# First batch of an FFT and FFN kernel: filter rows interleaved over the partitions, two filter units loaded twice, one product moved to GpSimd

## Chip, cores, metric

One core of one Trainium2 chip. The metric is the device time of one execution in microseconds (us); every time below is a median of several executions. Positions such as "at 38.09" are us from the start of the span of one profiled execution. SyncE, GpSimd, VectorE, ScalarE and TensorE are the engines; SPq in a profile is the instruction queue of SyncE, which here only issues DMA transfers.

## The reference, cut

```python
X = np.fft.rfft(x, axis=1)                       # x: 8 x 3008 x 256, float32
Y = X * (filt_r + 1j * filt_i)[None]             # filters: 1505 x 256 each, float32
y = np.fft.irfft(Y, n=3008, axis=1).reshape(24064, 256)
h = y @ w_in                                     # w_in: 256 x 2048
g = h * (1.0 / (1.0 + np.exp(-beta * h)))
out = g @ w_out                                  # w_out: 2048 x 256
```

## The kernel before, the parts that matter

The FFT is done as matmuls against tables that the kernel builds. The filtered spectrum of the first batch is made in six units of four frequency columns (`KU = 4`, `NUN = 6`). Each unit is matmuls (`s2_0`), two products on VectorE with the filters, and 16 more matmuls (`s3_0`, called by `unit`). Only when all six units are through can the FFN of the first batch start; from there TensorE runs to the end almost without a gap (0.84 us, the wait for xg). Filters are loaded once by SyncE, into one half of the 128 partitions, and copied to the other half by GpSimd (`spread`). Behind those copies, in the same GpSimd queue, stand the loads of w_in, and then of the second batch's rows (`load_x`, tile `xg`). The loads of w_out (tile `ws`) follow the filters in SyncE's queue.

```python
    def load_filters(k0, k1):                    # M = 64, H = 32
        n = k1 - k0
        for filt, dst, p0 in ((filt_r, fr_sb, M), (filt_i, fi_sb, 0)):
            for q0, off, sg in ((p0, k0, 1), (p0 + H, N1 - k0, -1)):
                src = AP(filt.tensor, filt.offset + off * D, [[N1 * D, H], [sg * D, n], [1, D]])
                nc.sync.dma_start(dst[q0 : q0 + H, k0:k1, :], src)
    # ... cut
    for u in range(NUN):
        load_filters(u * KU, (u + 1) * KU)
    # ... cut
    def s2_0(u):
        # ... cut: matmuls into ps
        nc.vector.tensor_tensor(pq[u, 0][:], ps[:], fr_sb[:, ks, :], ALU.mult)
        nc.vector.scalar_tensor_tensor(pq[u, 1][:], ps[:], rot[:], fi_sb[:, ks, :], ALU.mult, ALU.mult)
    # ... cut
    def spread(u):
        ks = slice(u * KU, (u + 1) * KU)
        nc.gpsimd.tensor_copy(fr_sb[:M, ks, :], fr_sb[M:, ks, :])
        nc.gpsimd.tensor_copy(fi_sb[M:, ks, :], fi_sb[:M, ks, :])
    # ... cut
    for u in range(4):
        spread(u)
    load_win(0, 4 * P)
    spread(4)
    load_win(4 * P, FF)
    spread(5)
    for g in range(4):
        load_x(1, g)
```

## Time and profile before

| | before |
|---|---|
| time | 782.33 us (782.07 to 782.78) |
| TensorE busy, whole span | 764.1 of 780.2 us |
| last of the 24 filter loads issued / landed | 22.29 / 26.70 |
| w_in loads issued | 23.40 and 26.37 |
| last product of the first batch ended | 30.61 |
| first FFN matmul | 33.84 |

### The profile page before, as it was taken

The numbers are of one execution on the slowest core, as the hardware profiler recorded it, in microseconds if no ns is written. First come the engines' busy times: TensorE is split into PE (matmuls) and PEld (weight loads), VectorE is DVE, ScalarE is ACT, GpSimd is POOL, SyncE is SP. The second block draws the span as 40 slices with busy tenths as digits, with TensorE's granted clock in tenths as the row PEclk, the third lists the DMA queues.
The fourth block names the chain that finished last, engine by engine and source line by source line (L and its number), as shares of the span: only waits on it lengthen the run. The fifth ranks groups of instructions, "written<-read, shape, count | busy, mean of one in ns | idle before, by whom it ended". The sixth has DMA issues, their size and how long they took to land.

```text
span 780.2 us, 15154 instructions
## 1 busy us (share of the span) xinstructions
PE 764.1 (98%) x5956; PEld 544.0 (70%) x6051; DVE 446.0 (57%) x713; ACT 552.6 (71%) x814; POOL 151.4 (19%) x155
## 2 busy tenths in 40 slices
PE   8899999999999999999999999999999999999997
PEld 5677667766776667866678666776667776676665
DVE  7869754766556665566546665567655666321001
ACT  6767877676677766777667776677766777777776
POOL 6714400312012210122201322022200222000000
PEclk9999999999999999999999999999999999999999
DMA  9975585244913358042671417622164111500101
GB/s 185 233 213 116 147 209 155 70 108 115 252 42 80 103 116 242 29 113 71 152 207 45 119 48 181 176 75 69 48 189 135 48 48 49 156 28 28 55 28 55
DMA packets 84411, 88.51 MB, mean 113 GB/s; under 512 B 5788, under 2 KB 74652, under 8 KB 84340
## 3 DMA queue, kind: packets, MB, share of 16 engines
q1 hardware_dynamic: 79892, 73.81, 32.0%
q0 software_dynamic: 4304, 13.60, 10.5%
q8 instruction: 47, 0.77, 0.4%
q14 instruction: 24, 0.20, 0.1%
q10 hardware_dynamic: 144, 0.13, 0.0%
HBM read 54.47 MB, written 46.66 MB: 130 GB/s over the span
## 4 chain that ended last, share of the span: by engine, by line
PE 94%; DMA 2%; issue 1%; POOL 1%; DVE 1%; SPq 0%; ACT 0%; DVEq 0%; POOLq 0%
PE acc L788 43%; PE hps L770 39%; PE ps L561 3%; PE ps L629 3%; PE ps L607 3%; PE ps L577 2%; DMA xg<-in_x_dram 1%; DMA fi_sb<-in_filt_i_dram 1%; POOL fi_sb L473 0%; POOL fr_sb L472 0%; SPq L91 0%; PE ps L405 0%; PE tp L400 0%; DVE y L114 0%; DVE u L224 0%
## 5 line engine op out<-in xcount | busy, mean ns | idle before, releaser
L779 ACT ACTIVATE gT<-hps,beta_sb 128x512 bf16<-128x512 f32 x752 | 516.9, 687 | 213.3 <-PE hps L770 191.9
L788 PE MATMUL acc<-wout_sb,gT 128*128 128x256 bf16 x3008 | 452.9, 272 | 2.3
L770 PE MATMUL hps<-y,win_sb 128*128 128x512 bf16 (+7 forms) x1636 | 428.0, 350 | 0.1
L788 PEld LDWEIGHTS <-gT 128*128 128x128 bf16 x3008 | 286.9, 98 | 121.6 <-issue 0.9
L596 POOL TENSOR_TENSOR yh<-a_t,b_t 128x512 bf16<-128x512 f32 x84 | 106.4, 1267 | 424.1 <-DVE b_t L595 422.8
L770 PEld LDWEIGHTS <-win_sb 128*128 128x128 bf16 x1728 | 164.8, 98 | 25.2 <-issue 0.9
L112 DVE COPY ost<-acc 128x512 f32<-128x512 f32 (+1 forms) x94 | 59.9, 679 | 138.3 <-PE acc L788 138.2
L112 DVE CAST a<-ps 96x512 bf16<-96x512 f32 x107 | 72.9, 685 | 53.3 <-PE ps L561 49.3
L114 DVE TENSOR_SCALAR y<-ps 128x376 bf16<-128x376 f32 (+2 forms) x128 | 63.3, 510 | 61.2 <-PE ps L629 57.9
L591 DVE TENSOR_TENSOR a_t<-ps,fr_sb 128x512 f32<-128x512 f32 x84 | 58.1, 692 | 67.0 <-PE ps L577 66.5
L592 DVE SCALAR_TENSOR_TENSOR b_t<-ps,fi_sb 64x512 f32<-64x512 f32 x84 | 58.2, 693 | 1.1
L595 DVE TENSOR_TENSOR b_t<-ps,fi_sb 64x512 f32<-64x512 f32 x84 | 57.4, 683 | 1.1
L112 DVE CAST z<-ps 128x512 bf16<-128x512 f32 x72 | 49.3, 684 | 1.7 <-PE ps L607 0.8
L629 PEld LDWEIGHTS <-zz 96*128 96x128 bf16 x448 | 29.7, 97 | 22.9
L561 PE MATMUL ps<-xg,t 94*96 94x512 bf16 x112 | 41.9, 381 | 1.5 <-DMA xg<-in_x_dram 0.8
L629 PE MATMUL ps<-t,zz 96*128 96x94 bf16 x448 | 34.7, 205 | 0.7
L607 PE MATMUL ps<-yh,t 128*128 128x256 bf16 x168 | 32.1, 273 | 0.6
L577 PE MATMUL ps<-a,t 128*128 128x256 bf16 x168 | 32.1, 273 | 0.3
L607 PEld LDWEIGHTS <-t 128*128 128x128 bf16 x168 | 16.2, 98 | 17.7 <-issue 0.7
L577 PEld LDWEIGHTS <-t 128*128 128x128 bf16 x168 | 16.1, 98 | 16.3
L171 POOL DMA_DIRECT2D xg<-in_x_dram x24 | 12.5, 521 | 56.7 <-PE ps L561 56.7
L561 PEld LDWEIGHTS <-t 94*96 94x96 bf16 x112 | 13.8, 123 | 10.3
(95 smaller groups left out, 177.3 us busy)
## 6 DMA issues: line engine op xcount, KB each, us to landing
out_dram<-ost SPq DMA_DIRECT2D x42, 512.0 KB, 3.0
d<-a SPq DMA_DIRECT2D x28, 384.0 KB, 5.1
a<-d SPq DMA_DIRECT2D x28, 384.0 KB, 4.9
d<-z SPq DMA_DIRECT2D x28, 384.0 KB, 3.9
zz<-d SPq DMA_DIRECT2D x28, 384.0 KB, 7.1
xg<-in_x_dram POOLq DMA_DIRECT2D x24, 384.0 KB, 6.3
out_dram<-ost SPq DMA_DIRECT2D x9, 256.0 KB, 3.8
ws<-in_moe_w_out_dram SPq DMA_DIRECT2D x4, 512.0 KB, 6.6
```

The source lines that it names most:

```text
L112: nc.vector.tensor_copy(dst, src)
L114: nc.vector.tensor_scalar_mul(dst, src, scale)
L561: nc.tensor.matmul(ps[:KP], lhsT=t1[:], rhs=xg[b, g][:NP, jj : jj + 2, :], start=True, stop=True)
L577: nc.tensor.matmul(ps[:, e, :], lhsT=t2[:, k0 + e, :], rhs=st["a2", b, g][:, kk + e, :], start=True, stop=True,)
L591: nc.vector.tensor_tensor(a_t[:], ps[:], fr_sb[:, ks, :], ALU.mult)
L592: nc.vector.scalar_tensor_tensor(b_t[:M], ps[M:], -1.0, fi_sb[M:, ks, :], ALU.mult, ALU.mult)
L596: nc.gpsimd.tensor_tensor(yh[:], a_t[:], b_t[:], ALU.add)
L607: nc.tensor.matmul(ps[:, e, :], lhsT=t3[:, 2 * i + e, :P], rhs=yh[:, e, :], start=True, stop=True)
L629: nc.tensor.matmul(ps[:, e, :NP], lhsT=zz[:, j0 % JG + e, dc * P : (dc + 1) * P], rhs=t4[:], start=True, stop=True,)
L770: nc.tensor.matmul(hps[:, pos - t0 : pos - t0 + ln], lhsT=win_sb[:, dc, fb * P : (fb + 1) * P], rhs=ys[b][:, dc, n0 : n0 + ln], start=(dc ...
L779: nc.scalar.activation(gT[:], hps[:], ACT.Silu, scale=beta_sb[:, fb : fb + 1])
L788: nc.tensor.matmul(acc_of(i, tb)[:, tb % 2, :], lhsT=blk[i * NFB + fb][:, tb * P : (tb + 1) * P], rhs=wout_sb[:, fb, :], start=(fb == 0 an ...
```

## The change

Its intent, as far as the code tells: write each filter load to every second of 64 partitions in place of 32 neighbouring ones (the frequency rows k and their mirrored rows are interleaved; the tables are reordered to match), take real and imaginary loads in turn, load the last two units straight into both halves so that GpSimd need not copy them and can issue w_in and xg earlier, give one product of the fifth unit to GpSimd, and shift the second batch's first steps by one so that TensorE meets xg later. The order of the calls of the units, and of the scaling of w_out on GpSimd, changes with it.

```diff
+    DUP = 2 * KH
+    def load_filters(k0, k1, halves):
+        for hi, off, sg in ((0, k0, 1), (1, N1 - k0, -1)):
+            for (filt, dst), p0 in zip(FILTERS, halves):
+                src = AP(filt.tensor, filt.offset + off * D, [[N1 * D, H], [sg * D, k1 - k0], [1, D]])
+                nc.sync.dma_start(dst[p0 + hi : p0 + M : 2, k0:k1, :], src)
 # ... cut: tables reordered, t2_shift by exclusive-or on pairs
-    for u in range(NUN):
-        load_filters(u * KU, (u + 1) * KU)
+    for u in range(DUP // KU):
+        load_filters(u * KU, (u + 1) * KU, (M, 0))
+    load_filters(DUP, NK, (M, 0))
+    load_filters(DUP, NK, (0, M))
 # ... cut
+        if on_pool:
+            nc.scalar.activation(zc[:], ps[:], ACT.Copy, scale=rot[:])
         nc.vector.tensor_tensor(pq[u, 0][:], ps[:], fr_sb[:, ks, :], ALU.mult)
+        if on_pool:
+            return
 # ... cut
     load_win(0, 4 * P)
-    spread(4)
     load_win(4 * P, FF)
-    spread(5)
-    for g in range(4):
-        load_x(1, g)
+    load_x(1, 0)
 # ... cut: order of the calls below
+    s2_0(4, True)
+    pool_product(4)              # two gpsimd.tensor_tensor of 128x512
+    for g in range(1, 4):
+        load_x(1, g)
 # ... cut: second batch
-            s1_steps(1, range(16), [1 + (2 * i + 1) // 3 for i in range(16)], False, (1, 4, 7, 10, 13))
-            for i, r in enumerate((11, 12, 13, 14)):
+            s1_steps(1, range(16), [2 + (2 * i + 1) // 3 for i in range(16)], False, (1, 4, 7, 10, 13))
+            for i, r in enumerate((2, 3, 4, 5)):
                 at(r, f_late, 1, i // 2, i % 2)
             for g in range(NG):
-                at(o + 13, a2_load, 1, g)
+                at(o + 14, a2_load, 1, g)
```

The number of filter loads stays 24: 16 of 128 KB for the first four units and 8 of 256 KB for the last two.

More of the change, by code (lines that the diff above doesn't have):

```diff
@@ L84 @@
     CH = M * J
-    def load_filters(k0, k1):
-        n = k1 - k0
-        for filt, dst, p0 in ((filt_r, fr_sb, M), (filt_i, fi_sb, 0)):
-            for q0, off, sg in ((p0, k0, 1), (p0 + H, N1 - k0, -1)):
-                src = AP(filt.tensor, filt.offset + off * D, [[N1 * D, H], [sg * D, n], [1, D]])
-                nc.sync.dma_start(dst[q0 : q0 + H, k0:k1, :], src)
+    FILTERS = ((filt_r, fr_sb), (filt_i, fi_sb))
+    DUP = 2 * KH
[4 more added lines that the diff above has]
+                nc.sync.dma_start(dst[p0 + hi : p0 + M : 2, k0:k1, :], src)
     t1 = consts.tile([NP, KP], BF16, name="t1", tag="t1")
@@ L184 @@
     load_x0(8, 16)
-    iota(vi[:, :, :H], [[1, NK], [N1, H]])
+    viv = vi[:].rearrange("p k (m h) -> p k m h", h=2)
+    iota(viv[:, :, :, 0], [[1, NK], [N1, H]])
     load_x0(16, 24)
-    iota(vi[:, :, H:], [[1, NK], [-N1, H]], base=N1 * (M - 1))
+    iota(viv[:, :, :, 1], [[1, NK], [-N1, H]], base=N1 * (M - 1))
     load_x0(24, 28)
@@ L218 @@
     q_i = shift_and("q_i", 0, 1)
-    v_i = shift_and("v_i", 5, 1)
     q_p = (affine("q0", q_i, -1.0, 1.0), affine("q1", q_i, 1.0, 0.0))
@@ L224, in t2_half @@
         nc.vector.tensor_scalar(
-            t[:], vi[:, :, hi * H : (hi + 1) * H], ms[:], off[:], ALU.mult, ALU.add
+            t[:], viv[:, :, :, hi], ms[:], off[:], ALU.mult, ALU.add
         )
@@ L228, in t2_half, with t2_shift @@
         nc.scalar.activation(
-            t2[:, :, hi * H : (hi + 1) * H], t[:], ACT.Sin, scale=TWO_PI / TURN
-        )
-    def t2_shift(hi):
-        for c in range(2):
+            t2[:, :, :M].rearrange("p k (m h) -> p k m h", h=2)[:, :, :, hi],
+            t[:],
+            ACT.Sin,
+            scale=TWO_PI / TURN
+        )
+    def t2_shift():
+        pairs = t2[:].rearrange("p k m -> p (k m)").bitcast(I32).rearrange("p (k m) -> p k m", k=NK)
+        for c, bit in enumerate((1 << 15, -(1 << 31))):
             d0, s0 = (0, M) if c == 0 else (M, 0)
-            dst = t2[d0 : d0 + M, :, M + hi * H : M + (hi + 1) * H]
-            src = t2[s0 : s0 + M, :, hi * H : (hi + 1) * H]
-            if c == hi:
-                nc.vector.tensor_scalar_mul(dst, src, -1.0)
-            else:
-                nc.vector.tensor_copy(dst, src)
+            nc.vector.tensor_scalar(
+                pairs[d0 : d0 + M, :, H:], pairs[s0 : s0 + M, :, :H], bit, None, ALU.bitwise_xor
+            )
     MG = 4
@@ L310 @@
     nc.sync.dma_start(seen[:], t2[:1, 1, M - 2 : M])
-    for u in range(NUN):
-        load_filters(u * KU, (u + 1) * KU)
+    for u in range(DUP // KU):
+        load_filters(u * KU, (u + 1) * KU, (M, 0))
+    load_filters(DUP, NK, (M, 0))
+    load_filters(DUP, NK, (0, M))
     gp = nc.gpsimd
-    rot = affine("rot", v_i, 2.0, -1.0, gp)
+    rot = affine("rot", q_i, 2.0, -1.0, gp)
     tiny = sp.tile([P, NFB], F32, name="tiny", tag="tiny")
@@ L321 @@
     spin(5, idle)
-    t2_shift(0)
-    t2_shift(1)
+    t2_shift()
     nc.vector.memset(t2[:, 0, M : P : M - 1], 0.0)
@@ L424, with s2_0 @@
     p0pool = rpool("p0pool", r_p0, bufs=2, **tw)
-    def s2_0(u):
+    zc = sr.tile([P, KU, D], F32, name="zc", tag="zc")
+    def s2_0(u, on_pool=False):
         ps = bank2([P, KU, D])
@@ L482, with pool_product @@
     load_win(0, 4 * P)
-    spread(4)
     load_win(4 * P, FF)
-    spread(5)
-    for g in range(4):
-        load_x(1, g)
+    load_x(1, 0)
+    def pool_product(u):
+        for i in range(0, KU, 2):
+            k0 = u * KU + i
+            nc.gpsimd.tensor_tensor(
+                pq[u, 1][:, i : i + 2, :], zc[:, i : i + 2, :], fi_sb[:, k0 : k0 + 2, :], ALU.mult
+            )
     load_wout(0)
     load_wout(WG)
-    scale_wout(0)
-    scale_wout(WG)
     s2_0(0)
@@ L500 @@
     s2_0(2)
+    a0_turn(4)
     unit(1)
-    a0_turn(4)
     s2_0(3)
+    a0_turn(5)
+    s2_0(4, True)
+    pool_product(4)
+    for g in range(1, 4):
+        load_x(1, g)
+    scale_wout(0)
+    scale_wout(WG)
     unit(2)
-    s2_0(4)
-    a0_turn(5)
     t3_part(2, True)
     t3_neg(2, True)
-    unit(3)
     s2_0(5)
@@ L512 @@
     spin(3, idle)
+    unit(3)
     unit(4)
```

## The prediction

> **What bounds the kernel now.** I read the stretches first (busy time of each engine in windows of the span), because shares over 780 us hide a short phase. Columns: window, its length, then busy us and count for PE, PEld, DVE, ACT, POOL, then the granted clock, DMA share, GB/s.
>
> ```profile
> 0.00:36.60 36.60, 30.08 (x340) 21.12 (x344) 30.29 (x56) 26.35 (x38) 27.26 (x41) 1.00 1.00 208
> 36.60:64.00 27.40, 27.18 (x231) 19.28 (x235) 19.30 (x42) 17.59 (x28) 3.79 (x2) 1.00 0.72 203
> 120.00:400.00 280.00, 278.21 (x2124) 198.09 (x2157) 175.24 (x271) 194.93 (x285) 51.95 (x49) 1.00 0.46 122
> ```
>
> From 36.6 us to the end TensorE has no idle time worth having (278.21 of 280). The change touches nothing there but the order of a few early pieces. So the time is "when does the steady stream begin" plus a constant, and the whole question is the first 36.6 us, where the DMA engines are full (share 1.00) while no compute engine is. Next the chain of waits, as start, length, what:
>
> ```profile
> 26.37 0.37 POOL win_sb L476
> 26.74 0.40 issue
> 27.14 1.03 POOL fr_sb L472
> 28.17 0.06 issue
> 28.23 0.39 POOL fi_sb L473
> 28.62 0.59 issue
> 29.21 7.35 DMA xg<-in_x_dram
> 36.56 0.04 issue
> 36.61 0.38 PE ps L561
> ```
>
> GpSimd copies the filters from one half of the partitions to the other (12 copies of 1.04 us), and behind the copies in its queue stand the loads of the FFN weights and of the second batch's rows (xg). xg is issued at 29.21, lands at 36.56, and TensorE waits 0.84 us for it at step 1. Beside it runs a second, nearly as long chain on VectorE, the two filter products of six units:
>
> ```profile
> 25.38 1.21 DVE L434 TENSOR_TENSOR pq_t<-sps,fr_sb 128x1024 bf16<-128x1024 f32 x1
> 26.52 1.27 DVE L435 SCALAR_TENSOR_TENSOR pq_t<-sps,rot,fi_sb 128x1024 bf16<-128x1024 f32 x1
> 28.20 1.22 DVE L434 TENSOR_TENSOR pq_t<-sps,fr_sb 128x1024 bf16<-128x1024 f32 x1 [0.41 <-POOL fr_sb L472]
> 29.34 1.27 DVE L435 SCALAR_TENSOR_TENSOR pq_t<-sps,rot,fi_sb 128x1024 bf16<-128x1024 f32 x1
> ```
>
> The products run back to back from 16.08, 2.32 us a unit, lose 0.41 us to the last GpSimd copy, and end at 30.61. The first FFN matmul follows at 33.84, and 2.7 us later TensorE stands before xg. Both chains must get shorter; either alone is worth at most the 0.84 us.
>
> Last, what the DMA engines do. The first line is the stretch from 15 to 24 us, filter loads alone; the second from 26 to 27 us, the load of w_out, 1 KB packets over 128 partitions:
>
> ```profile
> DMA packets 1510, 2.08 MB, mean 231 GB/s; under 512 B 250, under 2 KB 1254, under 8 KB 1510
> DMA packets 341, 0.33 MB, mean 334 GB/s; under 512 B 15, under 2 KB 341, under 8 KB 341
> ```
>
> Filters move at 231 GB/s although many of their packets are larger. In the packet records a 4 KB filter packet takes 159 ns when alone and about 300 ns in the crowded stretch; a 1 KB one 46 against about 70.[...]
>
> [...]
> [...]here GpSimd's 128x512 sum takes 1267 ns, and I use that.[...]
>
> **The change part by part.**
> 1. GpSimd loses four copies (units 4 and 5): 4 x 1.04 = 4.2 us before the x load. Copies of unit 3 still end near 23.4 to 23.9 (they follow the landing of the filters, 22.27 for unit 3), so both weight loads and the first x load (0.84 + 0.72 + 0.5) are issued by about 25.5 to 26 instead of 29.7. Since the DMA engines are full, the landing moves by less than the issue.
> 2. DMA gains 1.05 MB: units 4 and 5 twice. In units of 128 KB the filters go from 24 to 32. Before, these 24 took from about 12.0 to 25.7 us (one engine, about 1 us behind, ends at 26.7): 0.56 us each. Unchanged rate: 32 x 0.56 = 17.9, end 29.9, with the late engine 31, plus what the w_in load takes in between. At 300 GB/s (0.437 each): 14.0, end 26.0, late 27.0. At 382 (my ceiling from 2 x 159 + 8 x 46 ns for 16 KB on an engine): 11, end 23, late 24.
> 3. VectorE loses one 1.27 us product, unit 5's 0.41 us wait, and saves little in the table shift (two exclusive-ors on 64x768 words in place of four bf16 operations of 0.36 us; perhaps 0.1 to 0.2 us, hidden behind x arriving at 9.96). Six units then want to end at 16.08 + 6 x 2.32 - 1.14 = 28.9, if the filters are there.
> 4. ScalarE gains one scaled copy[...]; it has room, being idle 1.1 us before two later evacuations.
> 5. GpSimd gains two products of 1.27 us, 2.5 us, which need all the imaginary filters of unit 4, i.e. the last DMA of the filters. The first is ready at about 26.0 at best. They end at 28.6 (ceiling rate), at 29.6 (300 GB/s: 27.0 + 2.5), or at 33.6 and later (old rate).
> 6. TensorE meets xg one step later; a step without it (two matmuls of the first layer, 0.43, and eight transposes, 0.45) is 0.88 us, enough to cover the present wait of 0.84. The moved pieces load VectorE in steps 2 to 5 to about 1.9 us against 1.4 on TensorE; three PSUM buffers should absorb most of 2 us, so I put 0 to 0.4 us on it.
>
> Sum by filter rate, for the start of the steady stream, as the later of the product chain and xg. Ceiling: products end about 1.4 us earlier (after 28.6, two half units of matmul, 0.6 each), and the 0.85 us wait goes: -2.3. At 300: the products end about where they did (GpSimd at 29.6 to 30.0 holds up unit 4 and the last unit behind it), xg lands about 0.7 us later from the added bytes (14.0 against 13.3), and the step's shift gives 0.88: about -0.2 to -0.6. At 236: unit 4 waits to about 30, GpSimd to 33.6 or more, the start slips by 4.5 to 5, less 0.85: about +3.9.
>
> **The rivals.**
> (a) The added bytes cost more than GpSimd's copies: filters still at 231 to 245 GB/s, the last load after 30 us, a new VectorE wait on DMA before unit 4, time 784 to 786.[...] Against it: 4 KB packets did run at 159 ns in the first microsecond[...]; and nobody would buy 1 MB more without room.
> (b) Filters run near the ceiling, so that the x load lands by about 35 and the product chain sets the start: 780.0. For it: w_out ran at 334 GB/s right after.[...]
> (c) The GpSimd product becomes the last link: 2.5 us on an engine twice as slow as the 1.27 us it replaces. At middle rates this eats the gain, time 781.5 to 782.3. For it: it depends on the very last load. Against it: unit 4 is not the last unit, so about 1.2 us of slack lies behind VectorE's own last product.
> (d) Later effects (steps 2 to 5) give back up to 0.4 us; small.
>
> **Range and chances.** I expect a rate of 300 to 330 GB/s[...] and so -1.0 us: 781.3 us. The best case worked out above is -2.3 (780.0), the worst plausible +3.9 (786.2); I take 779.3 to 785.0 as eight in ten. 2% is 15.6 us; no rival comes near it, since the whole stage touched is 36.6 us and nothing in it is worth 15: 0.98 for within 2%, 0.01 each side.
>
> **What would show it.** Right: mean GB/s from 15 to 24 us above 290; no wait of unit 4's product for fr_sb over 0.5 us; win_sb issued before 24.5 and xg before 26; the TensorE wait for xg gone or under 0.3 us; first FFN matmul before 33.9; the rest unchanged in length. Wrong: a rate still near 231, VectorE idle for the filter DMA before its fifth product, the unit 4 matmuls released by GpSimd after 31 us, the first FFN matmul after 35; or a stretch of 36.6 to 64 us that became longer by more than 0.5 us, which would mean that the moved pieces stall TensorE.

The sum came to -2.3 us at the ceiling (382 GB/s), -0.2 to -0.6 at 300, and +3.9 at 236. The choice of 300 to 330 GB/s, and with it -1.0 us (781.3), was the author's estimate.

## More of the kernel before

The prediction shows the stretches and the chain of waits. Two more views matter for what follows. The first is SyncE's instruction queue in time order (start, length, engine, line, transfer, count): one filter load takes about half a microsecond to issue, pauses included, since each line holds two.

```profile
18.28 1.00 SPq L91 DMA_DIRECT2D fr_sb<-in_filt_r_dram  x2
19.42 1.01 SPq L91 DMA_DIRECT2D fi_sb<-in_filt_i_dram  x2
20.54 0.94 SPq L91 DMA_DIRECT2D fr_sb<-in_filt_r_dram  x2
```

The second is the DMA view of 15 to 20 us: packets, bytes, rate; then the queue's packets, MB and share of the 16 engines' time. The share counts the packets' times; I read 100% or more as engines that are always busy, so that they, not SyncE's issuing, limit the loads.

```profile
DMA packets 839, 1.17 MB, mean 234 GB/s; under 512 B 140, under 2 KB 692, under 8 KB 839
...
q1 hardware_dynamic: 839, 1.17, 106.0%
```

## The result

The changed kernel takes 794.48 us (793.58 to 795.64, 4 runs) against 782.33 (782.07 to 782.78, 4 runs): ratio 1.0156, 95% interval 1.0138 to 1.0173. A ratio here and below is the mean time of one kernel's runs over the mean of the other's of the same rounds, so not quite the ratio of the medians quoted. That is 12.2 us slower, far outside the predicted 779.3 to 785.0. "Within 2%" (15.6 us) was right, but not for its reason, "nothing in it is worth 15": the loss used up 12.2 of them.

The stretches after (columns as in the prediction: window, length, busy us and count of PE, PEld, DVE, ACT, POOL, then granted clock, DMA share, GB/s):

```profile
0.00:36.60 36.60, 24.20 (x265) 16.88 (x265) 23.40 (x39) 22.81 (x30) 17.95 (x32) 0.94 0.89 193
36.60:64.00 27.40, 23.20 (x192) 16.41 (x193) 15.77 (x33) 15.54 (x26) 11.55 (x9) 0.84 0.66 174
120.00:400.00 280.00, 280.00 (x2164) 197.94 (x2162) 176.21 (x272) 195.42 (x290) 51.92 (x49) 1.00 0.45 118
```

The steady stream is untouched (280.00 of 280). In the first 36.6 us TensorE and VectorE do about a fifth less than before, and the DMA engines, which had been full (1.00, 208 GB/s), now are at 0.89 and 193 GB/s although there is more to load. The chain of waits says what everything stood behind (start, length, what):

```profile
24.51 0.62 SPq L93
25.18 12.91 DMA fi_sb<-in_filt_i_dram
38.49 2.49 POOL pq_t L499 x2
41.03 0.82 PE sps L454 x6
41.85 1.71 PE lp L454 x16
43.56 1.85 PE zp L404 x16
...
46.95 0.59 PE hps L788 x2
```

One filter load is issued at 25.18, and its data are complete 12.9 us later; the two halves of the GpSimd product, a string of small matmuls and then the first FFN matmul follow at 46.95 (33.84 before). VectorE's and GpSimd's own timelines (the bracket is the idle time before, and what ended it):

```profile
24.52 1.27 DVE L445 SCALAR_TENSOR_TENSOR pq_t<-sps,rot,fi_sb 128x1024 bf16<-128x1024 f32 x1
33.65 2.35 DVE L442 TENSOR_TENSOR pq_t<-sps,fr_sb 128x1024 bf16<-128x1024 f32 x2 [7.86 <-issue]
38.26 1.28 DVE L445 SCALAR_TENSOR_TENSOR pq_t<-sps,rot,fi_sb 128x1024 bf16<-128x1024 f32 x1 [2.26 <-issue]
...
24.39 1.57 POOL L486 DMA_DIRECT2D win_sb<-in_moe_w_in_dram  x2
25.93 0.57 POOL L173 DMA_DIRECT2D xg<-in_x_dram  x1
38.49 2.48 POOL L499 TENSOR_TENSOR pq_t<-zc,fi_sb 128x512 bf16<-128x512 f32 x2 [11.99 <-DMA fi_sb<-in_filt_i_dram]
```

The first four units' products keep the old pace (the fourth's end at 25.79, 25.46 before). Then VectorE stands for 7.86 us until the fifth unit's real filters have landed at 33.38, and again for 2.26; GpSimd waits 11.99 us. The bracket's "issue" on VectorE only means that the profile shows no releaser; the landing just before tells which it was. Also note the two w_in loads, both issued by 26.0, within 0.8 us of the start of the last filter load's own issue.

SyncE's queue and the DMA view of 15 to 20 us, to be read against the same two views of before:

```profile
18.01 0.60 SPq L93 DMA_DIRECT2D fr_sb<-in_filt_r_dram  x1
18.66 0.59 SPq L93 DMA_DIRECT2D fi_sb<-in_filt_i_dram  x1
19.29 0.62 SPq L93 DMA_DIRECT2D fr_sb<-in_filt_r_dram  x1
```

```profile
DMA packets 719, 0.93 MB, mean 186 GB/s; under 512 B 107, under 2 KB 620, under 8 KB 719
...
q1 hardware_dynamic: 719, 0.93, 64.6%
```

The issue of a load to every second partition takes 0.60 us, where one to neighbouring partitions took about 0.42 (0.32 when it had waited). One starts every 0.65 us, and 131,072 bytes in 0.65 us are 202 GB/s: the DMA engines are busy only 64.6% of the time, and a 4 KB packet takes 159 ns (median from 15 to 24 us), 296 ns before. I read this as SyncE's issuing, not the transfer, being the limit; e13 and e14 test it. When the loads double in size (23 to 28 us), the DMA engines are always busy again (SyncE's queue has 103.8% of their time), and then its rate is 230 GB/s, as before the change.

Last, 32 to 36 us, when only the final filter loads are still to come: the queues' packets, MB and share.

```profile
DMA packets 471, 0.93 MB, mean 232 GB/s; under 512 B 24, under 2 KB 254, under 8 KB 471
...
q0 software_dynamic: 235, 0.70, 87.5%
q1 hardware_dynamic: 236, 0.23, 20.9%
```

GpSimd's queue q0 (w_in, 3 KB packets, and from 35.3 on some of xg's) and SyncE's q1 (filters, 1 KB packets) get nearly the same number of packets through, 235 and 236, so q0 gets three quarters of the bytes: the filters crawl at 58 GB/s. I read the equal counts as turns, packet by packet, in this stretch; they are not shown to be a rule (e4 from 32 to 36 us: 202 packets of q0 and 311 of q1).

So the theory is threefold: (T1) stepped partitions cost issue time (0.60 us a load for 0.42), so filters are late when their bytes double; (T2) the added 1.05 MB cost what they take at 230 GB/s; (T3) the filters, now late, meet w_in, which takes three quarters of the bytes (0.70 of 0.93 MB from 32 to 36 us). It is the filters that moved: the first packet of w_in ran at 28.68, 27.13 before (its first load was issued 1.0 us later than before, 24.39 for 23.40, only the second earlier, 25.22 for 26.37). Rivals: the interleaved transfer is slow in itself (R1); the GpSimd product is what costs (R2); the half clock that TensorE is granted from 31.87 on, for 13.65 us, is what costs (R3).

### The profile page after: what moved, and what is told of

Read it like the earlier page. It is cut to its first block, busy times and chain, and to the rows that moved or that the text cites. A ratio compares the mean times of both kernels' runs of the same rounds, so it can differ in the third digit from the quotient of the medians.

```text
span 791.8 us, 15243 instructions
## 1 busy us (share of the span) xinstructions
PE 771.0 (97%) x6051; PEld 545.9 (69%) x6051; DVE 444.6 (56%) x709; ACT 553.7 (70%) x815; POOL 149.8 (19%) x153
## 4 chain that ended last, share of the span: by engine, by line
PE 94%; SPq 2%; DMA 2%; DVE 1%; POOL 0%; issue 0%; ACT 0%; POOLq 0%
PE acc L806 42%; PE hps L788 41%; PE ps L579 3%; PE ps L647 2%; PE ps L625 2%; PE ps L595 2%; SPq L93 2%; DMA fi_sb<-in_filt_i_dram 2%; PE tp L404 0%; POOL pq_t L499 0%; PE ps L409 0%; PE zp L404 0%; PE lp L454 0%; DVE u L226 0%; DVE u L147 0%
## 5 line engine op out<-in xcount | busy, mean ns | idle before, releaser
L788 PE MATMUL hps<-y,win_sb 128*128 128x512 bf16 (+7 forms) x1728 | 447.9, 351 | 0.1
```

The costliest lines, as they stand in the source:

```text
L788: nc.tensor.matmul(hps[:, pos - t0 : pos - t0 + ln], lhsT=win_sb[:, dc, fb * P : (fb + 1) * P], rhs=ys[b][:, dc, n0 : n0 + ln], start=(dc ...
```

## The experiments

Fifteen kernels ran, all with correct results. "Left at w_in" is my own sum over the packet records: the filters' bytes that had not yet ended when the first w_in packet started (packets of SyncE's queue counted in order, so good to some 0.1 MB). For before it is zero: the last filter had landed at 26.70, and the first w_in packet ran at 27.13.

| kernel | time, us | ratio | left at w_in, MB | last filter landed | first FFN matmul |
|---|---|---|---|---|---|
| before | 782.3 | 1 | 0 | 26.70 | 33.84 |
| after | 794.48 | 1.0156 | 0.68 | 38.09 | 46.95 |
| e1_late_queue | 791.08 | 1.0103 | 0.71 | 34.52 | 43.39 |
| e2_win_1k | 789.84 | 1.0086 | 0.71 | 34.67 | 43.13 |
| e3_no_double | 787.60 | 1.0058 | 0.28 | 31.47 | 41.78 |
| e4_interleave_only | 786.63 | 1.0051 | 0.31 | 31.64 | 39.01 |
| e5_alternate_only | 782.27 | 1.0000 | 0 | 25.17 | 34.32 |
| e6_double_contiguous | 786.81 | 1.0060 | 0.08 | 31.16 | 40.02 |
| e7_kept_warm | 793.54 | 1.0141 | 0.69 | 38.43 | 45.84 |
| e8_steps_only | 781.61 | 0.9994 | 0 | 27.15 | 33.94 |
| e9_slow_issue | 782.79 | 1.0011 | 0.07 | not after 29.2 | 36.30 |
| e10_product_on_vector | 786.44 | 1.0052 | 0 | 29.75 | 38.16 |
| e11_best_alt_steps | 782.10 | 0.9998 | 0 | 24.95 | 33.87 |
| e12_best_act_copy | 781.55 | 0.9991 | 0 | 25.46 | 33.47 |
| e13_pace_065 | 784.81 | 1.0036 | 0.26 | 31.06 | 37.45 |
| e14_interleave_large | 784.00 | 1.0017 | 0 | 28.13 | 37.26 |
| e15_win_behind | 793.40 | 1.0152 | none met | 32.95 | 41.82 |

### Sharing with w_in: e1, e2, e15

e1: the changed kernel, with the second w_in load and all x loads behind the GpSimd products.

```diff
     load_win(0, 4 * P)
-    load_win(4 * P, FF)
-    load_x(1, 0)
 # ... cut
     pool_product(4)
-    for g in range(1, 4):
+    load_win(4 * P, FF)
+    for g in range(4):
         load_x(1, g)
```

> The changed kernel with only the order of GpSimd's queue altered: the second w_in load and all loads of the second batch's rows stand behind the two GpSimd products, so that nothing of GpSimd's but the first w_in load (256 KB) meets the filter loads. Theory A (the last filter loads, 1 KB packets, take turns packet by packet with w_in's 3 KB packets, which the shorter GpSimd queue issues too early): the last imaginary filter lands near 32 to 33 us instead of 38.1, the products end near 35, and although w_in and xg now come late (landing near 41 and 43) the kernel gains 4 to 7 us: 787 to 791. Theory B (the added megabyte by itself): filters still land near 38, w_in and xg even later, 796 to 800.

Measured 791.08 us (790.61 to 791.92), 95% interval of the ratio 1.0077 to 1.0129. The last filter landed at 34.52 for 38.09, and 3.4 us came back (medians, 794.48 less 791.08). That supports T3; the landing was later than the 32 to 33 I had expected, as I read it because the first w_in load still shared.

e2: the changed kernel, with the second w_in load cut in three, so that its packets have 1 KB. Bytes and place in the queue stay.

```diff
-    load_win(4 * P, FF)
+    for f0 in range(4 * P, FF, 4 * P):
+        load_win(f0, f0 + 4 * P)
```

> The changed kernel with the second w_in load (768 KB, 3 KB packets) cut into three of 256 KB (1 KB packets), same bytes, same place in the queue. Theory A (turns packet by packet): a filter packet waits for a third of the bytes, so the last filter lands near 35 instead of 38.1 and the time falls by about 3 us, 790 to 793. Theory B (bytes): same bytes, so 794 to 795 as the changed kernel.

Measured 789.84 us (789.26 to 790.36), interval 1.0055 to 1.0117, last landing 34.67. The packet size of the other queue fell, and 4.6 us came back. (Cut in three, w_in also took 3.0 us to issue for 1.57, and xg was issued at 27.35 for 25.93.) The queues from 30 to 34 us show the split directly, first in the changed kernel, then in e2: (nearly) equal counts in both, and with equal packets equal bytes.

```profile
q0 software_dynamic: 308, 0.66, 85.1%
q1 hardware_dynamic: 302, 0.30, 27.0%
```

```profile
q0 software_dynamic: 513, 0.49, 72.6%
q1 hardware_dynamic: 514, 0.49, 44.9%
```

e15: the changed kernel with both w_in loads behind the products, so that no w_in packet meets a filter packet.

```diff
-    load_win(0, 4 * P)
-    load_win(4 * P, FF)
-    load_x(1, 0)
 # ... cut
     pool_product(4)
-    for g in range(1, 4):
+    load_win(0, 4 * P)
+    load_win(4 * P, FF)
+    for g in range(4):
         load_x(1, g)
```

> The changed kernel with both loads of w_in and all loads of x issued behind the GpSimd products. If sharing with w_in is what makes the last landing late: 1.71 MB left at 24 us at 230 GB/s are 7.4 us, so the last filters land at 31.4 to 33 us (38.09 in the changed kernel, 34.52 in e1_late_queue). If the last loads are slow of themselves: 34 us or later. Time: the products would end near 35.5, but w_in is then issued only there, so the first FFN matmul comes no earlier than 42.5 and the time is 788.5 to 792.

The last landing, 32.95, is where T3 puts it: by this pair of traces, sharing with w_in cost 5.1 us of landing. The time, 793.4 us (790.61 to 796.81), is worse than expected. The filters were early, the first FFN matmul came at 41.82, but now w_in starts only behind the products, and TensorE next waited 2.6 us for xg. VectorE and GpSimd in time order:

```profile
31.97 2.35 DVE L442 TENSOR_TENSOR pq_t<-sps,fr_sb 128x1024 bf16<-128x1024 f32 x2 [6.34 <-issue]
...
35.78 1.56 POOL L486 DMA_DIRECT2D win_sb<-in_moe_w_in_dram  x2
37.34 2.08 POOL L173 DMA_DIRECT2D xg<-in_x_dram  x4
```

Moving the bytes behind repairs one wait and makes another: as I read it, these bytes must all move before the stage can end, whatever their order.

### The parts alone: e3, e4, e5, e6, e8

e3: the changed kernel, units 4 and 5 loaded once and copied by GpSimd as before the change.

```diff
-    for u in range(DUP // KU):
+    for u in range(NUN):
         load_filters(u * KU, (u + 1) * KU, (M, 0))
-    load_filters(DUP, NK, (M, 0))
-    load_filters(DUP, NK, (0, M))
 # ... cut
     load_win(0, 4 * P)
+    spread(4)
     load_win(4 * P, FF)
+    spread(5)
     load_x(1, 0)
```

> The changed kernel with units 4 and 5 loaded once and copied by GpSimd as before (24 loads of 128 KB, 12 copies); interleave, GpSimd product and step shift stay. Theories A and B: the filters land by 28, unit 4's product waits for no DMA[...], 782 to 784 (GpSimd's product behind its copies ends near 31.7, 1 us late, the step shift gives 1 us back). Theory C (the interleave itself is the loss): 788 or more.

787.60 us (787.07 to 788.44), interval 1.0032 to 1.0085, just short of what C said: with the doubled bytes gone, 4.9 us of the loss stay. So the bytes are not the only cause. (GpSimd's product now stands behind its copies in the queue, so this run is no clean sum of the other parts.)

e4: the kernel before with interleaved rows and alternated loads, nothing else.

```diff
+        for hi, off, sg in ((0, k0, 1), (1, N1 - k0, -1)):
+            for (filt, dst), p0 in zip(FILTERS, halves):
 # ... cut
+                nc.sync.dma_start(dst[p0 + hi : p0 + M : 2, k0:k1, :], src)
 # ... cut: tables reordered as in the change
```

> The kernel before with the interleaved layout alone (rows, tables, exclusive-or shift, alternated load order).[...] If it only makes each load slower to issue (0.60 us a load on the queue of SyncE against 0.42): a load every 0.65 us, about 200 GB/s, last filter near 27.5 instead of 26.7, unit 5 about 0.8 us later, 782.5 to 783.5.

(The alternative expected faster loads: above 290 GB/s, 780 to 781.5 us.)

786.63 us (785.05 to 789.95), interval 1.0016 to 1.0086: the direction is that of the issue theory, the size is not. I had expected the filters 0.8 us later; the last landed 5 us later, and from 26.6 on they shared with w_in (0.31 MB left). But this trace is of the slowest of e4's runs, and late filters are not all of it: at 49.25 TensorE stood 2.4 us for the scaled w_out, whose second load landed at 47.23 (30.52 before); the mean granted clock of that run was 0.992 (0.998 to 1.00 in the runs of the kernel before).

e5: the kernel before, real and imaginary loads alternated, rows contiguous.

```diff
-        for filt, dst, p0 in ((filt_r, fr_sb, M), (filt_i, fi_sb, 0)):
-            for q0, off, sg in ((p0, k0, 1), (p0 + H, N1 - k0, -1)):
+        for hi, off, sg in ((0, k0, 1), (H, N1 - k0, -1)):
+            for filt, dst, p0 in ((filt_r, fr_sb, M), (filt_i, fi_sb, 0)):
+                q0 = p0 + hi
```

> The kernel before with the load order alone changed: real, imaginary, real, imaginary to opposite halves of the partitions, rows contiguous as before.[...] If the 230 GB/s stays whatever the order: 225 to 240 GB/s, last filter 26.3 to 27.0, and 782 to 782.8 us. Issue time of a load stays 0.42 us in both; were it 0.60, the alternation and not the interleave would be what slows the issue.

(The alternative expected faster loads: 260 GB/s or more, last filter by 25.5.)

782.27 us (781.42 to 782.74), ratio 1.0000 (0.9985 to 1.0014). The alternation does help the loads: 246 GB/s from 15 to 20 us (234 before), with 95.6% of the engines' time, last landing 25.17 for 26.70. (The same order gave 268 GB/s in e11's trace and 257 in e12's.) It is worth no time; as I read it, VectorE's products and xg set the start, not the filters. The DMA view of 15 to 20 us:

```profile
DMA packets 866, 1.23 MB, mean 246 GB/s; under 512 B 149, under 2 KB 704, under 8 KB 866
```

e6: the changed kernel without the interleave (32 neighbouring partitions a load, tables as before); doubled loads, product on GpSimd and step shift stay.

```diff
-                nc.sync.dma_start(dst[p0 + hi : p0 + M : 2, k0:k1, :], src)
+                nc.sync.dma_start(dst[p0 + H * hi : p0 + H * hi + H, k0:k1, :], src)
 # ... cut: tables as before the change
```

> The changed kernel with contiguous partition halves (the interleave undone with its tables; double loads, GpSimd product, order and step shift stay). If the interleave's slower issue were the main loss: filters of units 0 to 3 land at 22 anyway (DMA rate), so the doubled loads still end late. I expect issue 0.42 us, units 0 to 3 landed by 22.3, the last filter at 35 to 38 since w_in still cuts in, 791 to 794.5. A time under 786 would put the loss on the interleave.

786.81 us (786.18 to 787.70), interval 1.0045 to 1.0075. I had expected 791 to 794.5, wrongly: without the interleave most of the loss is gone. The interleave costs 3.9 us alone (e4) and 7.7 on top of the doubled loads (794.48 less 786.81). The losses do not add: 3.9 and 4.5 make 8.4, and both together 12.2. The column "left at w_in" fits that: 0.31 and 0.08 MB become 0.68.

e8: the kernel before with the shift of the second batch's steps alone (the last block of the diff above).

```diff
-            s1_steps(1, range(16), [1 + (2 * i + 1) // 3 for i in range(16)], False, (1, 4, 7, 10, 13))
+            s1_steps(1, range(16), [2 + (2 * i + 1) // 3 for i in range(16)], False, (1, 4, 7, 10, 13))
```

> The kernel before with only the step shift (first-batch pieces into steps 2 to 5, second batch's first stage from step 2 on). My prediction's term: the wait for xg (0.84 us) goes, up to 0.4 us is given back in steps 2 to 5: 781.4 to 782.0. If the moved pieces stall TensorE by more: 782.3 or above.

781.61 us (781.38 to 782.38), ratio 0.9994 (0.9979 to 1.0009): not to be told from nothing. In the trace the first second-layer matmul came at 37.37 (37.69 before), but the 256th only at 106.41 (106.47): by these two traces, what was won at xg was given back within the moved steps. The wait for xg did not go either: 0.69 us, 0.84 before.

### Is the interleave slow by its issue? e9, e13, e14

e9: e5 with an 8-byte load after every second filter load, to slow the issue of contiguous loads.

```diff
+            i = 2 * (k0 // KU) + (hi > 0)
+            nc.sync.dma_start(tick[:, 2 * i : 2 * i + 2], filt_r[i : i + 1, :2])
```

> The alternated contiguous loads of e5_alternate_only, with one extra 8-byte load after every second filter load, so that the SyncE queue starts a filter load about every 0.65 us on the mean, as the interleaved kernel does, while the loads keep their fast form[...]. Theory A (the interleave costs by its slower issue alone): mean rate from 15 to 20 us near 190 to 205 GB/s, last filter landing 29 to 32 us, time 785 to 787, as e4_interleave_only. Theory B (the interleaved destination is slow in itself, in the transfer): the last landing stays under 28 us and the time 782 to 783.5.

782.79 us (782.10 to 784.69), interval 0.9999 to 1.0024. By its number this favours B, but the run did not reach its condition: one filter load in 0.58 us, not 0.65, and only 0.07 MB left when w_in came. Its other signs lean to A: 188 GB/s from 15 to 20 us, and a last landing near 29. Inconclusive; so two more.

e13: the same with an 8-byte load after three of every four filter loads.

```diff
 # ... cut: i counts the filter loads
+                if i % 4 < 3:
+                    nc.sync.dma_start(tick[:, 2 * i : 2 * i + 2], filt_r[i : i + 1, :2])
```

> As e9_slow_issue, but with an 8-byte load after three of every four filter loads, so that the contiguous, alternated loads start about every 0.65 to 0.68 us. If the pace of the issue is the whole cause: mean rate from 15 to 20 us 165 to 190 GB/s, the last filters landing between 29 and 32.5 us, first matmul of the FFN near 38 to 40, time 785 to 788 as e4_interleave_only (786.6). If the interleaved transfer is slow in itself: time under 784.2 and the first FFN matmul before 37.5.

784.81 us (783.43 to 787.35), interval 1.0021 to 1.0050, with 0.64 us a load. The rate from 15 to 20 us and the last landing are those of the interleaved e4 (183 for 184 GB/s, 31.06 for 31.64), with contiguous rows. DMA view of e13, then of e4, 15 to 20 us:

```profile
DMA packets 724, 0.91 MB, mean 183 GB/s; under 512 B 118, under 2 KB 629, under 8 KB 724
...
q1 hardware_dynamic: 724, 0.91, 61.6%
```

```profile
DMA packets 707, 0.92 MB, mean 184 GB/s; under 512 B 106, under 2 KB 608, under 8 KB 707
...
q1 hardware_dynamic: 707, 0.92, 63.7%
```

The time lies between the two expectations (the first FFN matmul, 37.45, just on the side of a slow transfer): pace alone costs 2.5 us where e4 lost 3.9. The intervals of e13 and e4 overlap, so the 1.8 us between their medians are not settled; e13's trace has no wait for w_out, e4's has 2.4 us.

e14: e4, with the filters of two units in one load from the third unit on: interleaved, but 256 KB an issue.

```diff
-    for u in range(NUN):
-        load_filters(u * KU, (u + 1) * KU, (M, 0))
+    for u0, u1 in ((0, 1), (1, 2), (2, 4), (4, 6)):
+        load_filters(u0 * KU, u1 * KU, (M, 0))
```

> As e4_interleave_only, with the filters of units 2 and 3 and of units 4 and 5 loaded in one call each (256 KB a load for 128 KB), so 16 loads for 24. If the pace of the issue is the whole cause: the rate from 18 to 23 us is 235 GB/s or more, the last filters land at 25.5 to 27.5 us, the first FFN matmul comes before 36 and the time is 782 to 784. If the issue time grows with the size (1.2 us a load) or the interleaved transfer is slow in itself: rate under 210, last landing after 29, time 785.5 or more.

The issue still took 0.62 us a load, and 18 to 23 us ran at 261 GB/s with the engines full, faster than before the change. SyncE's queue, and the DMA view:

```profile
18.64 0.61 SPq L93 DMA_DIRECT2D fr_sb<-in_filt_r_dram  x1
```

```profile
DMA packets 697, 1.30 MB, mean 261 GB/s; under 512 B 74, under 2 KB 604, under 8 KB 604
...
q1 hardware_dynamic: 697, 1.30, 101.9%
```

So R1 falls: interleaved rows move as fast as contiguous ones (246 to 268 GB/s in e5, e11 and e12) when enough bytes are issued. The time, 784.00 us (783.11 to 784.55, interval 1.0004 to 1.0030), is at the upper edge of what was expected, and the landing (28.13) and the first FFN matmul (37.26) are later than expected: VectorE waited 2.42 us for the third unit, as I read it because the first two units still load slowly and a larger load lands later as a whole (5.5 us from issue to landing for real filters of 256 KB, 2.9 for 128 KB).

### The product on GpSimd, the clock: e10, e7

e10: e6 with the fifth unit's second product back on VectorE.

```diff
-    s2_0(4, True)
-    pool_product(4)
+    s2_0(4)
```

> The kernel e6_double_contiguous (786.81) with the second product of the fifth unit back on VectorE, so no product on GpSimd and no scaled copy on ScalarE. Theory A (the product on GpSimd is neutral: it frees VectorE for 1.27 us but takes 2.5 us itself and ends as late): 786.4 to 787.4. Theory B (the product on GpSimd is a loss, because all matmuls of the last two units then stand behind it): 785.0 to 786.2. Theory C (it is a gain): 787.6 or more.

786.44 us (785.05 to 787.49), interval 1.0039 to 1.0065, against e6's 1.0045 to 1.0075: neutral, as A said. R2 falls, at least where the filters land near 30. It also bears on T2. Against e5, with the same order of loads and contiguous rows, its last filter landed 4.6 us later (29.75 for 25.17), which is what 1.05 MB take at 230 GB/s. It costs 4.2 us, but that is no clean price of late filters: e10 keeps the step shift and the changed order of units and queues, which no run isolates, and its trace has a second wait, at 48.3 us for the scaled w_out, whose second load landed at 46.31 (30.52 before); e6's trace has 0.9 us of it, the changed kernel's none. Waiter, releaser, us in total, times, longest:

```profile
PE acc L805 <- POOL wout_sb L378: 2.1, 1, 2.1
```

e7: the changed kernel with dummy matmuls in TensorE's idle time (38 for 3, and 18 more), so that its clock stays up.

```diff
-    spin(3, idle)
+    spin(38, idle)
     unit(3)
+    spin(18, idle)
     unit(4)
```

> The changed kernel with TensorE kept busy by dummy matmuls in its two long waits (38 and 18 in place of 3). All waits stay. If the half clock (granted 0.50 from 31.9 to 45.5 us) costs what the stretch from the end of the products to the first FFN matmul grew by (6.0 against 3.2 us): 2.5 to 3 us faster, 791.3 to 792. If that stretch is long for another reason (w_in landing): no change, 794 to 795.

The granted clock stayed at 1.00, and the time is 793.54 us (791.77 to 794.36), interval 1.0124 to 1.0157: about 1 us better by the medians, not the 2.5 or more that I had expected, and not clear of noise (the changed kernel's interval is 1.0138 to 1.0173). From the end of the products to the first FFN matmul it takes 4.5 us, 6.0 in the changed kernel and 3.2 before. R3 is at most a small part. The windows of the changed kernel, then of e7 (the number after the five busy columns is the clock):

```profile
41.00:44.00 3.00, 2.97 (x27) 2.77 (x28) 0.41 (x2) 1.68 (x3) 3.00 (x4) 0.50 0.57 85
```

```profile
41.00:44.00 3.00, 2.23 (x37) 2.06 (x38) 1.15 (x3) 1.75 (x4) 3.00 (x5) 1.00 0.54 66
```

At half clock 27 matmuls take 2.97 us; at full clock 37 take 2.23. In the changed kernel's first 64 us the half clock was one stretch of 13.65 us, from 31.87 to 45.52.

### Can the good parts beat both kernels? e11, e12

e11: the kernel before with e5's alternation and e8's step shift (their two diffs together).

> The kernel before with two parts only: real and imaginary loads alternated (contiguous rows) and the shift of the second batch's steps by one. Alone they gave 0.0 and -0.5 us. If they add: 781.0 to 781.8. If the earlier landing of the filters (25.2 for 26.7 us) is worth something once the wait for the x load is out of the way: 780.0 to 781.0. If neither counts: 782.0 to 782.6.

782.10 us (781.06 to 783.25), ratio 0.9998 (0.9985 to 1.0010): neither counts.

e12: e11, with the copy of the sixth unit's real filters moved from GpSimd to ScalarE.

```diff
-        nc.gpsimd.tensor_copy(fr_sb[:M, ks, :], fr_sb[M:, ks, :])
+        if u < NUN - 1:
+            nc.gpsimd.tensor_copy(fr_sb[:M, ks, :], fr_sb[M:, ks, :])
 # ... cut
+    nc.scalar.activation(fr_sb[:M, ks5, :], fr_sb[M:, ks5, :], ACT.Copy)
```

> e11_best_alt_steps with the copy of the sixth unit's real filters moved from GpSimd to ScalarE, so that GpSimd issues the x load about 1 us earlier and VectorE's wait of 0.41 us for that copy goes. If the product chain sets the start: about 0.4 us under e11, 780.5 to 781.5. If ScalarE's copy delays an evacuation instead: equal to e11 or up to 0.5 us over it.

781.55 us (781.17 to 784.28), ratio 0.9991 (0.9977 to 1.0005): within noise of before, so no proven winner. The chains of waits of e11 and of e12 (that of before is in the prediction) show xg's issue and the time to its landing:

```profile
28.98 8.38 DMA xg<-in_x_dram
```

```profile
28.21 9.65 DMA xg<-in_x_dram
```

Issued at 29.21, 28.98 and 28.21, xg lands at 36.56, 37.36 and 37.86: the earlier issue, the later landing. So GpSimd's copies, which the prediction named as the head of this chain, did not set when xg landed in these traces; I take it to be the traffic beside it, and w_out as the likely rival, since it starts earlier when the filters end earlier, but no run isolates it. Of e12 the trace shows only its slowest run: TensorE waited 2.1 us for xg there, and then two matmuls with w_in took 0.85 us (from 39.65), 0.43 in e11, so it does not say what the median was made of.

## Why the prediction was wrong, point by point

It failed at step 2, twice: at the filter rate (300 to 330 GB/s expected, 205 measured from 15 to 24 us), and at the sharing with w_in, which the step names ("plus what the w_in load takes in between") and gives no number. Three of the signs that it gave for being wrong came true: VectorE idle before the fifth product (7.86 us), unit 4's matmuls released by GpSimd after 31 us (40.97), the first FFN matmul after 35 (46.95).

1. *GpSimd issues earlier.* Right as to time: w_in was out by 25.9 (at 24.39 and 25.22), the first xg at 25.93, as "by about 25.5 to 26" said. It bought nothing: xg, issued 3.3 us earlier, landed 3.1 us later (39.66 for 36.56), and the first w_in packet ran 1.55 us later than before. Before, no filter was left when it ran; now the filters were late and met it. That this sharing costs time is shown by e1, e2 and e15. Whether the copies taken off GpSimd's queue made it worse no run isolates; with all copies in the queue, e3 and e4 had 0.28 and 0.31 MB left too.
2. *Filters at 300 to 330 GB/s.* Measured 186 GB/s while the loads were small, 230 when doubled. The higher rate was the author's estimate. What it lacked is issue time: one 128 KB load every 0.65 us puts a ceiling of about 200 GB/s on the stream (131,072 bytes in 0.65 us are 202), however fast the transfer is. It priced DMA by packets and never asked how often SyncE starts one. Its 4 KB packets of 159 ns "when alone" were real, but they came back as the mark of a starved queue (64.6% of the engines' time from 15 to 20 us), not of a fast one. One reading was loose as well: that the trace of before had no loads to both halves at once. A load took about 4.5 us from issue to landing and one started every 0.56, so some eight were in flight at once, in both halves.
3. *VectorE saves 1.27 and 0.41 us.* It did less work, and then stood 7.86 and 2.26 us for filters, as the text under "what would show it wrong" says.
4. *The scaled copy on ScalarE has room.* The copy took 1.15 us; plain copies of 1024 took 1.02 in the kernel before. Nothing contradicts the step: e6 and e10 differ by it and the GpSimd product, and are equal within noise.
5. *GpSimd's product takes 2.5 us.* 2.48. Its start was the error: it ended at 40.97, where the worst case worked out was "33.6 and later".
6. *The step shift covers the xg wait, 0 to 0.4 us given back.* In the changed kernel the first FFN matmul is 13.1 us later and the first second-layer matmul 11.8, so 1.27 were won between them (the wait itself was 0.84; I take the rest to be work moved behind); 0.27 went back by the 256th. In e8, where xg still had to be waited for (0.7 us), it is worth nothing that four runs can show.

Rival (a) was the right one in kind, with "784 to 786" for 794.5; the range ended at 785.0 and so left out even the prediction's own worst case, 786.2. Its missing 8 us can be counted. The last landing moved by 11.39 us. Of that, the bytes: 1.05 MB at 230 GB/s, 4.6. The pace of issue: at 24 us the changed kernel had 1.71 MB still to come, e6 with the same bytes 1.19; 0.52 MB at 230 GB/s are 2.3. The sharing: 38.09 less 32.95 (e15), 5.1. Together 12.0, 0.6 more than the 11.39 seen; the first two are estimates from these records, the third a difference of two runs. From there on, in differences of the two traces: products end 2.88 after the landing for 3.91, -1.0; from there to the first FFN matmul 5.98 for 3.23, +2.8 (about half of it the clock, by e7's trace; the rest I put down to more matmuls behind the last product, as no run isolates it); the xg wait and what was given back, -1.0. The sum, 11.39 - 1.03 + 2.75 - 1.27 + 0.27, is 12.1; TensorE's last matmul is 12.11 us later; these are positions in the same two traces, so that they add up is no check of the causes. So the byte term, 4.6, is near the "4.5 to 5" that the prediction gave for the old rate, and 7.4 us of landing came from two terms that its sum did not price.

## What to carry to other kernels

Before a load is reshaped, read how long its issue takes and divide the bytes of one load by it: if that is near the rate, the queue that issues can be the next bound (here 202 GB/s by issue, 230 by transfer). Before a transfer is made longer or slower, or another is started earlier, ask which bytes of another queue it will then meet, and with what packet size: here the 3 KB packets took three quarters of the bytes from the 1 KB ones. Two small losses that push one transfer into another can cost more than their sum (12.2 us for 3.9 and 4.5), and the single parts will not show it. And look past the first wait: loads that move later can bring a second one, as w_out did in e4, e6 and e10.

## What else the traces show

- The issue of a load by SyncE, by the shape of its destination: 128 KB to 32 neighbouring partitions took 0.42 us (0.32 after a wait), to every second of 64 partitions 0.60, and 256 KB to the latter 0.62 (e14).
- Two queues with different packets: with 3 KB against 1 KB the split was 0.70 to 0.23 MB (235 against 236 packets, changed kernel), with 1 KB each 0.49 to 0.49 (513 against 514, e2), and cutting one load in three for 1 KB packets was worth 4.6 us.
- The first packet of a second queue: w_in, issued at 24.39, had its first packet 4.3 us later, at 28.68; in the kernel before 3.7 us (23.40 and 27.13). In e4, where SyncE's queue took 71.6% of the engines' time from 24 to 26 us, it came after 1.6 us. No run isolates the cause.
